# Attention over a long cache with a token mixer, on one core: the sixteenth query tile of a pair of heads loaded in six, six and four rows, and for two more pairs

## The chip, the core and the metric

The kernel runs on one core of one Trainium2 chip. The metric is the device time of one execution in microseconds (us), as the median of several executions. The core has engines for matrix products (PE, with PEld for its weight loads), for vectors (DVE), for activations (ACT), a general one (POOL), and a queue engine (SP) that issues nearly all loads from the chip's memory (HBM) into the on-chip memory. A load is carried out by up to 16 DMA engines side by side. The on-chip memory and the matrix results both have 128 rows, called partitions.

## The reference

Two layers, each an attention block with a residual and a mixer over one token with a residual. The batch is 2, one new token per batch entry, the width D is 512, and the cache holds 32768 positions for 8 key/value heads of 128 elements; four query heads share each of them. All data are 32-bit floats.

```python
q = (x @ wq).reshape(B, Sq, 32, 128).transpose(0, 2, 1, 3)
scores = einsum("bhqd,bhkd->bhqk", q, repeat(k_cache, 4)) * 128 ** -0.5
o = einsum("bhqk,bhkd->bhqd", softmax(scores), repeat(v_cache, 4))
attention = o.transpose(0, 2, 1, 3).reshape(B, Sq, 4096) @ wo
h = layernorm(y); u = gelu(einsum("bsd,sf->bdf", h, w1) + b1)
mixer = (einsum("bdf,fs->bds", u, w2) + b2).transpose(0, 2, 1)
# per layer: x = x + attention(layernorm(x)); x = x + mixer(layernorm(x))
```

The two caches are 268 MB each, and each layer reads both, apart from the parts that the kernel keeps on chip between the layers.

## The kernel before

**Units and chunks.** A unit is one layer, one batch entry and one key/value head (`units`, 32 in all). A unit's keys and values are read in chunks of 4096 positions (2 MB); usually four chunks come in one load of 8 MB (128 rows of 64 KB), so that a unit has two loads of keys and two of values. The script (`load_only`, `use`, `through`, `usual`) lists loads and uses in one fixed order: four key chunks of unit n, four value chunks of unit n-1, and so on. One use of a chunk is one step of the kernel's own clock (t); `kbeg[n]` is the step at which unit n's keys begin. `at(time, f, ...)` hangs any other work on such a step, so all orders are fixed when the program is built, and every engine runs its instructions in that order. SP waits, in order, for the buffer of the next load to come free (cells 0 to 7 of `mem`, of 16 KB in each partition).

**Weights.** The query and output weights of two neighbouring heads (`TWO_HEADS`, pairs 0 to 3) come in one load into two cells from `WCELL0 + k % 2 * 2` on (`load_weights`, L115 to L122), ten steps before the first unit of the pair. A head has four query tiles and four output tiles of 128 x 512 values, that is 256 KB each; a pair has 16 tiles, 4 MB. In layer 0 the pairs come as 0, 1, 2, 3 (pair 3 holds head 6, `single`, and the keeper, head 7); in layer 1 head 6 comes first, with a load of its own (L1069), and then pairs 0, 1, 2.

**The low tile.** For the pairs in `PART`, 1 and 2, the fourth query tile of the pair's first head is left out of that load, which then has 15 tiles (3840 KB). Its 128 rows of weights are laid out differently in HBM (`_two_heads`): 32 rows of 2048 values (8 KB), each of which holds four of the 128 rows. They go to partitions 0 to 15 and 32 to 47 of cell 8 (`lower_tile`, L124 to L135), after DVE has cleared these 48 partitions (L130). Each pair takes eight loads of four rows, the rows four apart (`u`, `u + 4`, `u + 8`, `u + 12`), spread over steps 46 to 18 before the pair, one every four steps. `lower_input` (L137) gathers the matching input columns, once a layer, and `low_products` (L148) forms the four products of 48 rows that take the place of the one product of 128 rows in `q_products` (L311). `make_q` (L329) turns the finished query row into the columns that the key products read.

**The change of layers.** Between the layers (`changes`, `change_of_layer`) the keeper's units run with many small loads, some data stay on chip, and cells 8 to 12 hold keys and values for a time; the last key chunks of unit (1, 0, 6) lie in cells 8 and 9. Pair 0 of layer 1 is opened at the first unit after the two of head 6.

Of the kernel before, what the change touches and what calls it, by code (L numbers as in the profile page):

```python
# [13 lines left out]
P = 128  # L14
CK = 4096
# [7 lines left out]
BANKS = 3  # L23
KEPT_Q = 4
TWO_HEADS = ((0, 1), (2, 3), (4, 5), (6, 7))
PART = (1, 2)
Q = 16
SIXTEENS = (0, 1, 4, 5)
PIECES = (32, 16, 8, 4, 4)
THIN = 16  # L30
QT = 4
# [9 lines left out]
def gqa_mixer_kernel(ctx: ExitStack, tc: tile.TileContext, x, kt, v, wqo, cols, out):  # L41
# [17 lines left out]
    nc = tc.nc  # L59
    B, D = out.shape  # L60
# [4 lines left out]
    R = wqo.shape[2] // (4 * D)  # L65
    DT = D // P
# [28 lines left out]
    WCELL0, WCELLS = 9, 4  # L95
# [3 lines left out]
    home = {}  # L99
    mem = const.tile([P, (WCELL0 + WCELLS) * CK + REST * QT * DH], F32, name="mem")  # L100
# [4 lines left out]
    lowered = {}  # L105
    low, first_half = (sm["ln"][: 3 * Q, 16 + k : 16 + k + w] for k, w in ((0, len(SIXTEENS) * B), (len(SIXTEENS) * B, 1)))

# [4 lines left out]
        w = home[h] + (DT - (h in lowered)) * D  # L112
        return mem[:, w : w + W].rearrange("p (t c) -> p t c", t=R)

    def load_weights(k, cell, n=2):  # L115
        tiles = n * (DT + R) - (k in PART)
        for j in range(n):
            home[TWO_HEADS[k][j]] = cell * CK + j * (DT + R - (k in PART)) * D
        of = wqo[k]
        if k in PART:  # L120
            of = of.rearrange("p c -> (p c)")[: P * tiles * D].rearrange("(p c) -> p c", p=P)
        nc.sync.dma_start(mem[:, cell * CK :][:, : tiles * D], of[:, : tiles * D])  # L122

    def lower_tile(k, step):  # L124


        w = len(SIXTEENS) * D
        to = mem[: 3 * Q, (WCELL0 - 1) * CK + PART.index(k) * w :][:, :w]
        if step < 0:
            nc.vector.memset(to, 0.0)  # L130
            return
        lowered[TWO_HEADS[k][0]] = to
        of = wqo[k].rearrange("p c -> (p c)")[-P * D :].rearrange("(u c) -> u c", u=2 * Q)
        a, u = divmod(step, 4)
        nc.sync.dma_start(to[2 * Q * a + u : 2 * Q * a + Q : 4], of[Q * a + u : Q * a + Q : 4])  # L135

    def lower_input():  # L137


        p = misc()  # L140
        for j, a in enumerate(SIXTEENS):
            nc.tensor.matmul(
                p[: 3 * Q, j * B : (j + 1) * B], ident[:, a * Q : (a + 3) * Q], sm["xn"][:, -B:], start=True, stop=True
            )
        nc.vector.tensor_reduce(first_half, mask[: 3 * Q, :], axis=AX.X, op=ALU.add)
        nc.vector.tensor_scalar_mul(low, p[: 3 * Q, : len(SIXTEENS) * B], first_half)

# [151 lines left out]
    def unit_of(n):  # L299

        return units[n]
# [74 lines left out]
    def load(is_v, n, c, m, places=None):  # L376
# [7 lines left out]
        for t in bufs:  # L384
            for w in [w * P for w in PIECES] if last else (t.shape[-1],):
                nc.sync.dma_start(t[:, :w], src[:, f : f + w])
# [533 lines left out]
    n = X0  # L920
# [40 lines left out]
    n = Y1 + 1  # L961
# [12 lines left out]
    kbeg, k_done, vbeg, v_done, vend_of, t = {}, {}, {}, {}, {}, 0  # L974
# [16 lines left out]
    def at(time, f, *a, rank=1, **k):  # L991
        done.setdefault(time, []).append((rank, f, a, k))

    HC = NCH // HALVES
    opens = {two[0]: k for k, two in enumerate(TWO_HEADS)}
# [92 lines left out]
    for n in range(NU):  # L1088
        layer, b, h = unit_of(n)
        kend, vend = kend_of[n], vend_of[n]  # L1090
        ahead = vend_of[n - 1] if n else 0
        if n and not X0 < n <= Y1 + 1:
            q0 = kbeg[n] - 6
            q1, q2, q3 = q0 + 1, q0 + 2, q0 + 2
            apart = n != X0 and h not in opens
            if apart and layer == 1:
                at(kbeg[n] - 11, make_q, n, 4)
                at(q0, make_q, n, 5)
                at(q1, make_q, n, 6)
            else:  # L1100
                at(kbeg[n] - 11 if apart else q0, make_q, n, 0)
                at(q1, make_q, n, 1)
            at(q2, make_q, n, 2)
            at(q3, make_q, n, 3)
        if n and h in opens and b == 0 and h != single or units[n] == (0, 0, single):
            at(kbeg[n] - 10, load_weights, opens[h], WCELL0 + opens[h] % 2 * 2)
            if opens[h] in PART:
                at(kbeg[n] - 55, lower_tile, opens[h], -1)
                for step in range(8):
                    at(kbeg[n] - 46 + 4 * step, lower_tile, opens[h], step)  # L1110
                if opens[h] == PART[0]:
                    at(kbeg[n] - 17, lower_input)
                at(kbeg[n] - 11, low_products, n, 0, 1)
                at(kbeg[n] - 10, low_products, n, 2, 3)
        if not X0 < n <= Y1:
            last = n == NU - 1
            e = kend + 2
            t0 = max(k_done[n, HC - 1], *(v_done[n - 1, c] for c in range(HC) if n), 0)
            t1 = ahead if last else max(kend + 2, ahead + (2 if n == X0 else 4))
            at(max(kend, e - 1), max_1, n)  # L1120
            at(e, max_2, n)
            at(t0, turn_scores, n, 0)
            at(e, exponentials, n, 0)
            at(t1, turn_scores, n, 1)
            at(t1, exponentials, n, 1)
            at(t1 + (1 if last else 2), denominators, n)
        if n == NU - 1:
            at(t1 + 1, gelu_table)
            at(t1, last_rows, (layer, b))
            at(vend, last_out, n)  # L1130
            at(vend, last_mixer, n)
            continue
        if X0 <= n < Y1:
            continue
        assert vbeg[n + 1] >= vend
        at(min(vend + 1, vbeg[n + 1]), out_0, n)
        at(min(vend + 1, vbeg[n + 1]), out_1, n)
        at(vend if n == NU - 2 else vend + 2, out_2, n)
        if n == X0 - 1:
            at(vend + 2, fold_rows)  # L1140
        key = (layer, b)
        if units[n] == [u for u in units if u[:2] == key][-1]:
            at(vend, mix_1, key)
            at(vend + 2, take_rows, key, row_tile())
            at(vend + 3, mix_2, key)
            at(vend + 1, gelu_table)
            begin = vend + 3
            exps = [kend_of[m] + 2 for m in (n + 1, n + 2)]
            exps += [max(e, vend_of[m] + 4) for e, m in zip(exps, (n, n + 1))]
            when = [w for w in range(begin, begin + FT + 1 + len(exps)) if w not in exps][: FT + 1]  # L1150
            e = when.pop()
            for f, w in enumerate(when):
                at(w + 1, hidden_out, key, f, rank=0)
                at(w, hidden_tile, key, f, rank=2)
            at(e, take_rows, key, None, rank=2)
            at(e + 1, mix_4, key)
# [26 lines left out]
def _two_heads(two, parted, d):  # L1183

    import numpy as np

    if not parted:
        return np.concatenate(two, axis=1)
    c = np.arange((d // P - 1) * d, d // P * d)
    main = np.concatenate([np.delete(two[0], c, axis=1), two[1]], axis=1)  # L1190
    last = two[0][:, c]
    low = [np.concatenate([last[16 * a + u : 16 * a + u + 16] for a in SIXTEENS], axis=1) for u in (0, 32)]
    return np.concatenate([a.ravel() for a in (main, *low)]).reshape(P, -1)


def _layout(A_x, A_k_cache, A_v_cache, A_wq, A_wo, B_w1, B_b1, B_w2, B_b2):

    import numpy as np

    B, HKV, SK, DH = A_k_cache.shape  # L1200
    D = A_x.shape[-1]
    n = SK // CK


    keys = np.arange(SK).reshape(n, CK)
    for c0, m in GROUPS:
        keys[c0 : c0 + m] = keys[c0 : c0 + m].reshape(P, m, CK // P).transpose(1, 0, 2).reshape(m, CK)
    k = keys.reshape(n // PACK, PACK // 2, 2, NG, 32, JT // QT, QT // SUB, SUB)
    k = k.transpose(0, 1, 6, 7, 3, 2, 5, 4).reshape(n, CK)
    kt = np.empty((B * HKV, SK * DH), A_k_cache.dtype)  # L1210
    for u, a in enumerate(A_k_cache.reshape(B * HKV, SK, DH)):
        for c0, m in GROUPS:
            kt[u, c0 * CK * DH : (c0 + m) * CK * DH] = a[k[c0 : c0 + m].ravel()].T.ravel()
    wq = A_wq.reshape(D // P, P, HKV, -1).transpose(2, 1, 0, 3)
    wo = A_wo.reshape(HKV, -1, DH, D).transpose(0, 2, 1, 3)
    wqo = np.concatenate([wq.reshape(HKV, P, -1), wo.reshape(HKV, DH, -1)], axis=2)
    w2 = B_w2.reshape(P, -1)
    w2 = np.stack([np.zeros_like(w2), w2], axis=2)
    cols = [a.reshape(P, -1) for a in (B_w1, B_b1, w2)] + [np.broadcast_to(B_b2.reshape(1, 1), (P, 1))]
    return {  # L1220
        "x": np.ascontiguousarray(A_x.reshape(B * (D // P), P).T),
        "kt": kt,
        "v": A_v_cache.reshape(B * HKV, SK * DH),
        "wqo": np.stack([_two_heads([wqo[h] for h in two], k in PART, D) for k, two in enumerate(TWO_HEADS)]),
        "cols": np.concatenate(cols, axis=1),
    }

# [24 lines left out]
```

## Time and profile before

| | |
|---|---|
| three executions | 2483.12, 2483.34 (median), 2483.51 us |
| the profiled execution's own time | 2483.2 us |
| its span, first to last instruction | 2481.4 us |
| PE, DVE, ACT busy | 55%, 10%, 7% of the span |
| read from HBM | 1059.10 MB, 427 GB/s over the span |
| weight loads | 3 of 4096 KB, 4 of 3840 KB, 1 of 2048 KB, 32 of 32 KB |

How to read it: "busy" counts an engine's own instructions. The queue part of the page gives the packets of each DMA queue, their bytes, and the time that they took as a share of what 16 DMA engines have in the span. A row of a timeline gives the start in us from the span's start, the duration, the engine, the line, the operation with output and inputs, the count of instructions that were merged, and in brackets the idle time before it with what ended that idle time: "9.69 <-DMA mem<-in_kt_dram" is 9.69 us idle, ended by the landing of keys. SPq is SP's queue; its rows are the moments at which a load is issued, not the time of the transfer.

### The profile page before, as it was taken

What the parts mean: (1) busy time and instruction counts of PE and PEld (TensorE: products, weight loads), DVE (VectorE), ACT (ScalarE), POOL (GpSimd) and SP (SyncE); (2) the same over time, 40 slices, a digit from 0 to 9 for tenths busy, and PEclk for the clock granted to TensorE, in tenths of its full rate; (3) what the DMA queues carried; (4) which work ended last, traced back from release to release, by engine and by line L of the source; (5) the groups of instructions that cost most, each with busy time, mean ns of one, the idle gap of its engine ahead of it and who ended that gap; (6) DMA issues with size and microseconds to landing.
All of it is one profiled execution on the core that took longest, in us unless ns stands there. A gap on an engine that the chain in (4) does not pass through costs nothing.

```text
span 2481.4 us, 20712 instructions
## 1 busy us (share of the span) xinstructions
PE 1375.6 (55%) x9414; PEld 375.6 (15%) x9414; DVE 257.8 (10%) x665; ACT 185.7 (7%) x546; POOL 4.9 (0%) x17
## 2 busy tenths in 40 slices
PE   4545545556555455466788454555455454456556
PEld 1111111111111111111222111111111111111112
DVE  1000000000000000010334000000000000010002
ACT  0000000000000000000212000000000000011002
POOL 0000000000000000000000000000000000000000
PEclk8777777776777777778899877777777777777778
DMA  9999999999999999999999999999999999999996
GB/s 422 435 430 427 439 432 431 433 432 430 435 430 432 436 425 436 434 433 421 415 418 426 433 434 436 430 435 433 428 433 428 437 429 434 432 433 429 432 434 293
DMA packets 27570, 1060.44 MB, mean 427 GB/s; under 512 B 3413, under 2 KB 3417, under 8 KB 4570
## 3 DMA queue, kind: packets, MB, share of 16 engines
q1 hardware_dynamic: 27192, 1059.08, 99.2%
q8 instruction: 74, 1.21, 0.2%
q14 instruction: 14, 0.11, 0.0%
q10 hardware_dynamic: 290, 0.04, 0.0%
HBM read 1059.10 MB, written 0.00 MB: 427 GB/s over the span
## 4 chain that ended last, share of the span: by engine, by line
DMA 72%; PE 26%; DVE 1%; issue 0%; another core or an unknown queue 0%; ACT 0%; SPq 0%; POOL 0%; DVEq 0%; ACTq 0%
DMA mem<-in_v_dram 69%; PE acc L516 21%; DMA mem<-in_kt_dram 3%; PE score L417 2%; PE kept L155 1%; PE kept L321 0%; DVE acc L798 0%; PE small L548 0%; PE small L444 0%; PE bcast L417 0%; PE small L686 0%; PE small L438 0%; PE bcast L321 0%; PE kept L738 0%
## 5 line engine op out<-in xcount | busy, mean ns | idle before, releaser
L417 PE MATMUL score<-mem,small_sb 128*32 128x512 f32 x4032 | 600.1, 721 | 575.3 <-DMA mem<-in_kt_dram 574.5
L516 PE MATMUL acc<-mem,S 128*16 128x512 f32 x4088 | 602.5, 722 | 474.4 <-DMA mem<-in_v_dram 472.7
L417 PEld LDWEIGHTS score<-mem,small_sb 128*32 128x32 f32 x4032 | 139.2, 127 | 948.9 <-DMA mem<-in_kt_dram 595.0
L455 ACT ACTIVATE S<-S,small_sb 128x128 f32<-128x128 f32 x236 | 121.5, 518 | 2076.0 <-DVE small_sb L446 1417.1
L516 PEld LDWEIGHTS acc<-mem,S 128*16 128x16 f32 x4088 | 130.8, 108 | 812.3 <-issue 727.8
L430 DVE TENSOR_REDUCE small_sb<-score 128x1 f32<-128x512 f32 x63 | 43.6, 692 | 757.1 <-PE score L417 757.1
L450 DVE STREAM_TRANSPOSE S<-score 128x512 f32<-128x512 f32 x63 | 44.8, 711 | 131.2 <-PE acc L516 127.0
L321 PE MATMUL kept<-mem,small_sb 128*2 128x512 f32 x104 | 55.5, 655 | 1.7 <-DVE small_sb L267 1.7
L239 PE MATMUL kept<-mem,small_sb 128*1 128x512 f32 (+1 forms) x252 | 44.9, 599 | 2.6 <-ACT mem L781 2.4
L455 ACT ACTIVATION_READ_ACCUMULATOR S<-S,small_sb 128x1 f32 x236 | 44.1, 187 | 0.0
L440 DVE TENSOR_REDUCE small_sb<-small 1x4 f32<-1x128 f32 x32 | 8.9, 279 | 324.5 <-PE small L438 324.5
L550 DVE RECIPROCAL small_sb<-small 128x4 f32<-128x4 f32 x32 | 5.9, 185 | 311.6 <-PE small L548 311.6
L569 DVE TENSOR_TENSOR small_sb<-small,small_sb 128x4 f32<-128x4 f32 x30 | 4.9, 164 | 307.2 <-PE small L558 307.2
L486 DVE SCALAR_TENSOR_TENSOR S<-acc,small_sb,S 128x128 f32<-128x128 f32 x96 | 33.7, 351 | 3.4
L347 PE MATMUL small<-small_sb,mem 2*128 2x2 f32 x120 | 16.0, 251 | 19.3 <-DVE mem L343 19.3
L484 DVE TENSOR_SCALAR S<-acc,small_sb 128x128 f32<-128x128 f32 x32 | 11.2, 350 | 112.7 <-PE acc L516 112.7
L558 PEld LDWEIGHTS small<-small_sb,S 128*128 128x128 f32 x64 | 13.2, 258 | 49.6 <-issue 42.0
L347 PEld LDWEIGHTS small<-small_sb,mem 2*128 2x128 f32 x120 | 14.7, 189 | 33.3 <-DVE mem L343 30.0
L155 PE MATMUL kept<-mem,small_sb 48*2 48x512 f32 x32 | 18.7, 711 | 0.0
L438 PE MATMUL small<-small_sb 128*1 128x128 f32 x64 | 16.8, 357 | 3.0 <-DVE small_sb L436 3.0
L558 PE MATMUL small<-small_sb,S 128*128 128x4 f32 x64 | 16.0, 320 | 3.9 <-DVE S L486 3.9
L686 PE MATMUL small<-small_sb 128*128 128x128 f32 x102 | 16.9, 297 | 0.0
(177 smaller groups left out, 343.5 us busy)
## 6 DMA issues: line engine op xcount, KB each, us to landing
mem<-in_v_dram SPq DMA_DIRECT2D x13, 2048.0 KB
mem<-in_kt_dram SPq DMA_DIRECT2D x20, 1024.0 KB
mem<-in_kt_dram SPq DMA_DIRECT2D x4, 4096.0 KB
mem<-in_wqo_dram SPq DMA_DIRECT2D x4, 3840.0 KB
mem<-in_v_dram SPq DMA_DIRECT2D x15, 1024.0 KB
mem<-in_wqo_dram SPq DMA_DIRECT2D x3, 4096.0 KB
mem<-in_v_dram SPq DMA_DIRECT2D x3, 4096.0 KB
mem<-in_kt_dram SPq DMA_DIRECT2D x1, 6144.0 KB
```

The lines of the kernel that those rows point to most:

```text
L155: nc.tensor.matmul(q_ps[n][:B, :], low[:, j * B : (j + 1) * B], lowered[h][:, j * D : (j + 1) * D], start=(j == 0), stop=False,)
L239: nc.tensor.matmul((rows if to is None else to)[32 * g : 32 * g + b + 1, :], weights if b else weights[:, 1:], row, start=to is not None, ...
L321: nc.tensor.matmul(q_ps[n][:m, :], xnT[:, d, b : b + m], wq_at(h, d), start=(d == 0 and h not in lowered), stop=(d == last),)
L347: nc.tensor.matmul(pt[:, r * m : (r + 1) * m], q_row[n][:m, r * DH : (r + 1) * DH], ident[:m, :m], start=True, stop=True,)
L417: nc.tensor.matmul(sc_ps[n, half][32 * g : 32 * g + 32, :], q, kc[k * NG + g], start=first, stop=last,)
L430: nc.vector.tensor_reduce(mx[n][:, half : half + 1], sc_ps[n, half], axis=AX.X, op=ALU.max)
L450: nc.vector.transpose(S[half][:, :w], sc_ps[n, half][:, :w])
L455: nc.scalar.activation(s[:, :, h], s[:, :, h], AF.Exp, bias=neg[n][:, h : h + 1], scale=SCALE, accum_out=lsum[n][:, half, h : h + 1],)
L486: nc.vector.scalar_tensor_tensor(t, acc[:, k * DH : (k + 1) * DH], mask[:, k : k + 1], t, op0=ALU.mult, op1=ALU.add)
L516: nc.tensor.matmul(acc[32 * g : 32 * g + R * QT, :], S[half][:, col : col + R * QT], vc[q], start=((n, c) in v_first and q < NG), stop=((n ...
L558: nc.tensor.matmul(po[:, :R], blocks[n], selh, start=True, stop=True)
L686: nc.tensor.matmul(p[:, :P], ident, ident, start=True, stop=True)
```

## The change

`PART` becomes pairs 1, 2 and 3. The low tile's 16 rows on each side are loaded as rows 0 to 5, 6 to 11 and 12 to 15, neighbouring rows in each load (`SPLIT`), so a pair takes six loads of 6, 6, 4, 6, 6 and 4 rows.

Pair 3 has its low tile in layer 0, and pair 0 in layer 1. Pair 0 of layer 0 and head 6 of layer 1 keep the whole load; so two pairs are needed in both layouts, and HBM gets second copies of pairs 0 and 3 (`COPIES`, `source`). The 15-tile load is now put at the end of its two cells, not at the start. Of cell 8, odd pairs take the second half and even pairs the first.

For pair 0 of layer 1 (`near`) the places differ: DVE's clearing 16 steps before the pair, the six loads at steps 15, 14, 13, 11, 10 and 9 before, the low products at 4 and 3.5 before, the other three query products and the turning of the query at 3, 2.5, 2 and 1.5 before.

```diff
-PART = (1, 2)
+PART = (1, 2, 3)
+COPIES = (0, 3)
+SPLIT = ((0, 6), (6, 12), (12, 16))
...
-    def load_weights(k, cell, n=2):
-        tiles = n * (DT + R) - (k in PART)
+    def source(k, whole):
+
+        if whole == (k not in PART):
+            return wqo[k]
+        return wqo[len(TWO_HEADS) + COPIES.index(k)]
+
+    def load_weights(k, cell, n=2, whole=True):
+
+        tiles = n * (DT + R) - (not whole)
+        to = (cell + n) * CK - tiles * D
         for j in range(n):
-            home[TWO_HEADS[k][j]] = cell * CK + j * (DT + R - (k in PART)) * D
-        of = wqo[k]
-        if k in PART:
+            home[TWO_HEADS[k][j]] = to + j * (DT + R - (not whole)) * D
+        of = source(k, whole)
+        if whole:
+            lowered.pop(TWO_HEADS[k][0], None)
+        else:
             of = of.rearrange("p c -> (p c)")[: P * tiles * D].rearrange("(p c) -> p c", p=P)
-        nc.sync.dma_start(mem[:, cell * CK :][:, : tiles * D], of[:, : tiles * D])
+        nc.sync.dma_start(mem[:, to:][:, : tiles * D], of[:, : tiles * D])
...
-        to = mem[: 3 * Q, (WCELL0 - 1) * CK + PART.index(k) * w :][:, :w]
+        to = mem[: 3 * Q, (WCELL0 - 1) * CK + k % 2 * w :][:, :w]
...
-        of = wqo[k].rearrange("p c -> (p c)")[-P * D :].rearrange("(u c) -> u c", u=2 * Q)
-        a, u = divmod(step, 4)
-        nc.sync.dma_start(to[2 * Q * a + u : 2 * Q * a + Q : 4], of[Q * a + u : Q * a + Q : 4])
+        of = source(k, False).rearrange("p c -> (p c)")[-P * D :].rearrange("(u c) -> u c", u=2 * Q)
+        a, u = divmod(step, len(SPLIT))
+        u0, u1 = SPLIT[u]
+        nc.sync.dma_start(to[2 * Q * a + u0 : 2 * Q * a + u1], of[Q * a + u0 : Q * a + u1])
...
+            near = layer == 1 and opens.get(h) == 0 and b == 0
             q0 = kbeg[n] - 6
             q1, q2, q3 = q0 + 1, q0 + 2, q0 + 2
+            if near:
+                q0, q1, q2, q3 = (kbeg[n] - k / 2 for k in (6, 5, 4, 3))
...
-            at(kbeg[n] - 10, load_weights, opens[h], WCELL0 + opens[h] % 2 * 2)
-            if opens[h] in PART:
-                at(kbeg[n] - 55, lower_tile, opens[h], -1)
-                for step in range(8):
-                    at(kbeg[n] - 46 + 4 * step, lower_tile, opens[h], step)
-                if opens[h] == PART[0]:
+            k = opens[h]
+            whole = k == 0 and layer == 0
+            at(kbeg[n] - 10, load_weights, k, WCELL0 + k % 2 * 2, whole=whole)
+            if not whole:
+                at(kbeg[n] - (16 if near else 55), lower_tile, k, -1)
+                for step in range(2 * len(SPLIT)):
+                    i = step + step // len(SPLIT)
+                    at(kbeg[n] - 15 + i if near else kbeg[n] - 46 + 4 * step, lower_tile, k, step)
+                if k == 1 - layer:
                     at(kbeg[n] - 17, lower_input)
-                at(kbeg[n] - 11, low_products, n, 0, 1)
-                at(kbeg[n] - 10, low_products, n, 2, 3)
+                at(kbeg[n] - (4 if near else 11), low_products, n, 0, 1)
+                at(kbeg[n] - (3.5 if near else 10), low_products, n, 2, 3)
```

**SP, layer 0, ahead of pair 3.** Before, the rows up to the weights of pair 3 (the last row) are:

```order
L386 DMA mem<-in_kt_dram 128x16384
L386 DMA mem<-in_v_dram 128x16384
L386 DMA mem<-in_kt_dram 128x16384
L386 DMA mem<-in_v_dram 128x16384
L122 DMA mem<-in_wqo_dram 128x8192
```

Now, from the fourth of the six low loads on, there stands:

```order
L148 DMA mem<-in_wqo_dram 6x2048
L399 DMA mem<-in_kt_dram 128x16384
L148 DMA mem<-in_wqo_dram 6x2048
L399 DMA mem<-in_v_dram 128x16384
L148 DMA mem<-in_wqo_dram 4x2048
L399 DMA mem<-in_kt_dram 128x16384
L399 DMA mem<-in_v_dram 128x16384
L399 DMA mem<-in_kt_dram 128x16384
L399 DMA mem<-in_v_dram 128x16384
L134 DMA mem<-in_wqo_dram 128x7680
```

Six low loads have come in between the loads of keys and values, and the load of the pair's weights has 7680 values a row instead of 8192.

**SP, layer 1, ahead of pair 0.** Before, after the last key chunks of unit (1, 0, 6) (the three loads of 128x8192), there stands:

```order
L386 DMA mem<-in_kt_dram 128x8192 x3
L386 DMA mem<-in_kt_dram 128x16384
L386 DMA mem<-in_v_dram 128x16384
L122 DMA mem<-in_wqo_dram 128x8192
L386 DMA mem<-in_kt_dram 128x16384
L386 DMA mem<-in_v_dram 128x16384
```

Now:

```order
L399 DMA mem<-in_kt_dram 128x8192 x3
L399 DMA mem<-in_kt_dram 128x16384
L148 DMA mem<-in_wqo_dram 6x2048 x2
L148 DMA mem<-in_wqo_dram 4x2048
L399 DMA mem<-in_v_dram 128x16384
L148 DMA mem<-in_wqo_dram 6x2048
L134 DMA mem<-in_wqo_dram 128x7680
L148 DMA mem<-in_wqo_dram 6x2048
L148 DMA mem<-in_wqo_dram 4x2048
L399 DMA mem<-in_kt_dram 128x16384
L399 DMA mem<-in_v_dram 128x16384
```

Three low loads have come ahead of a value load, in whose issue SP must therefore first wait for DVE's clearing of cell 8.

**PE, layer 1, the query of pair 0's first unit.** Before, the four query products (L321) and the turning of the row (L347) stand among the last key products of the unit ahead (score_86):

```order
L417 MATMUL score_86<-mem,small_sb 32x512 x16
L321 MATMUL kept_82<-mem,small_sb 2x512 x2
L417 MATMUL score_86<-mem,small_sb 32x512 x8
L321 MATMUL kept_82<-mem,small_sb 2x512 x2
L417 MATMUL score_86<-mem,small_sb 32x512 x8
L347 MATMUL small<-small_sb,mem 128x2 x4
L516 MATMUL acc<-mem,S_90 16x512 x8
```

Now they stand among its last value products (acc), and the four low products (L168) ahead of them:

```order
L430 MATMUL score_86<-mem,small_sb 32x512 x32
L168 MATMUL kept_82<-mem,small_sb 2x512 x2
L529 MATMUL acc<-mem,S_90 16x512 x4
L168 MATMUL kept_82<-mem,small_sb 2x512 x2
L529 MATMUL acc<-mem,S_90 16x512 x4
L451 MATMUL small<-small_sb 1x128
L334 MATMUL kept_82<-mem,small_sb 2x512 x2
L529 MATMUL acc<-mem,S_90 16x512 x4
L334 MATMUL kept_82<-mem,small_sb 2x512
L529 MATMUL acc<-mem,S_90 16x512 x4
L457 MATMUL small<-small_sb 128x4
L529 MATMUL acc<-mem,S_90 16x512 x4
```

The query's work has moved behind the landing of the unit's last values, and the turning of the row follows the last of these rows.

More of the change, by code (lines that the diff above doesn't have):

```diff
@@ L113, in wo_at @@
         return mem[:, w : w + W].rearrange("p (t c) -> p t c", t=R)
-    def load_weights(k, cell, n=2):
-        tiles = n * (DT + R) - (k in PART)
-        for j in range(n):
-            home[TWO_HEADS[k][j]] = cell * CK + j * (DT + R - (k in PART)) * D
-        of = wqo[k]
-        if k in PART:
+    def source(k, whole):
[5 more added lines that the diff above has]
+        to = (cell + n) * CK - tiles * D
+        for j in range(n):
+            home[TWO_HEADS[k][j]] = to + j * (DT + R - (not whole)) * D
[3 more added lines that the diff above has]
+        else:
             of = of.rearrange("p c -> (p c)")[: P * tiles * D].rearrange("(p c) -> p c", p=P)
-        nc.sync.dma_start(mem[:, cell * CK :][:, : tiles * D], of[:, : tiles * D])
+        nc.sync.dma_start(mem[:, to:][:, : tiles * D], of[:, : tiles * D])
     def lower_tile(k, step):
         w = len(SIXTEENS) * D
-        to = mem[: 3 * Q, (WCELL0 - 1) * CK + PART.index(k) * w :][:, :w]
+        to = mem[: 3 * Q, (WCELL0 - 1) * CK + k % 2 * w :][:, :w]
         if step < 0:
+            lowered[TWO_HEADS[k][0]] = to
             nc.vector.memset(to, 0.0)
             return
-        lowered[TWO_HEADS[k][0]] = to
-        of = wqo[k].rearrange("p c -> (p c)")[-P * D :].rearrange("(u c) -> u c", u=2 * Q)
-        a, u = divmod(step, 4)
-        nc.sync.dma_start(to[2 * Q * a + u : 2 * Q * a + Q : 4], of[Q * a + u : Q * a + Q : 4])
+        of = source(k, False).rearrange("p c -> (p c)")[-P * D :].rearrange("(u c) -> u c", u=2 * Q)
+        a, u = divmod(step, len(SPLIT))
+        u0, u1 = SPLIT[u]
+        nc.sync.dma_start(to[2 * Q * a + u0 : 2 * Q * a + u1], of[Q * a + u0 : Q * a + u1])
     def lower_input():
@@ L1223, in _layout @@
         "v": A_v_cache.reshape(B * HKV, SK * DH),
-        "wqo": np.stack([_two_heads([wqo[h] for h in two], k in PART, D) for k, two in enumerate(TWO_HEADS)]),
+        "wqo": np.stack(
+            [
+                _two_heads([wqo[h] for h in TWO_HEADS[k]], parted, D)
+                for k, parted in [(k, k in PART) for k in range(len(TWO_HEADS))] + [(k, k not in PART) for k in COPIES]
+            ]
+        ),
         "cols": np.concatenate(cols, axis=1),
```

## The prediction

> **What bounds the kernel now.** I read the engine table and the queues first, then the chain, then the places where PE waits for loads.
>
> ```profile
> span 2481.4 us, 20712 instructions
> PE 1375.6 (55%) x9414; PEld 375.6 (15%) x9414; DVE 257.8 (10%) x665; ACT 185.7 (7%) x546; POOL 4.9 (0%) x17
> q1 hardware_dynamic: 27192, 1059.08, 99.2%
> q8 instruction: 74, 1.21, 0.2%
> DMA 72%; PE 26%; DVE 1%; issue 0%; another core or an unknown queue 0%; ACT 0%; SPq 0%; POOL 0%; DVEq 0%; ACTq 0%
> ```
>
> SP's queue, q1, keeps 16 DMA engines busy for 99.2% of the span, 2461.5 us each on average. Keys and values are read whatever the change does, so it can only alter how evenly these engines finish. The last landing shows how much there is to gain:
>
> ```profile
> 2463.75 1.06 PE L532 MATMUL kept<-mem,S 128*4 128x128 f32 x24 [0.24 <-DMA mem<-in_v_dram]
> 2465.06 0.40 PE L532 MATMUL kept<-mem,S 128*4 128x128 f32 x8 [0.25 <-DMA mem<-in_v_dram]
> 2478.88 0.58 SPq L769 DMA_DIRECT2D out_dram<-mem  x1
> ```
>
> The last wait for values ends at 2465.1 us, 3.6 us after the average engine's 2461.5. That is the most that better sharing could save (0.14%); the 16 us behind it are the closing mixer, which the change doesn't touch. So **a large gain is ruled out**.
>
> From the queue's row one engine moves 1059.08 MB / (16 x 2461.5 us) = 26.9 KB per us: 0.305 us for a row of 8 KB, and 0.61 us for its sixteenth of a 256 KB tile.
>
> **What the low loads cost now.** They go with every key and value load of a stretch. PE's waits for keys, in a stretch of layer 0 with a low load to every load, and in a later one without:
>
> ```profile
> 393.52 3.64 PE L417 MATMUL score<-mem,small_sb 128*32 128x512 f32 x16 [9.69 <-DMA mem<-in_kt_dram]
> ...
> 550.92 3.64 PE L417 MATMUL score<-mem,small_sb 128*32 128x512 f32 x16 [10.03 <-DMA mem<-in_kt_dram]
> ...
> 637.49 3.62 PE L417 MATMUL score<-mem,small_sb 128*32 128x512 f32 x16 [8.80 <-DMA mem<-in_kt_dram]
> ...
> 753.64 6.57 PE L417 MATMUL score<-mem,small_sb 128*32 128x512 f32 x44 [7.33 <-DMA mem<-in_kt_dram]
> ```
>
> The first two rows are four pairs of loads apart: 39.35 us a pair. The last two are three pairs apart: 38.72. The difference, 0.63 us, is that of two low loads: 0.317 us each, one 8 KB row on one engine (0.305 above). I read two things from it. A load of four rows uses four engines, one row each; and in this stretch those engines are the last of the sixteen, so what they carry is the pace. In layer 1 it begins otherwise:
>
> ```profile
> 1570.63 3.64 PE L417 MATMUL score<-mem,small_sb 128*32 128x512 f32 x16 [9.44 <-DMA mem<-in_kt_dram]
> ...
> 1609.34 5.80 PE L417 MATMUL score<-mem,small_sb 128*32 128x512 f32 x32 [9.37 <-DMA mem<-in_kt_dram]
> ...
> 1648.24 3.42 PE L417 MATMUL score<-mem,small_sb 128*32 128x512 f32 x16 [9.08 <-DMA mem<-in_kt_dram]
> ...
> 1687.31 9.51 PE L417 MATMUL score<-mem,small_sb 128*32 128x512 f32 x64 [10.10 <-DMA mem<-in_kt_dram]
> ```
>
> 38.71, 38.90 and 39.07 us: the first low loads are free, because other engines are later there, and then they come onto the path.
>
> **The change part by part.** *Rows and tiles.* Per layer it goes from two pairs with eight low loads to three with six. The engines that carry a row of every load pay 18 x 0.317 = 5.71 us, not 5.07: +0.63. All sixteen lose a sixteenth of one tile: -0.61. So the engines now last come out at **+0.02 us a layer**, and those without low rows at -0.61. What the layer gains depends on who is last at its end: +0.02 if it is the four engines of the low rows all along, -0.61 if others are. Over two layers that is +0.04 to -1.22. I take -0.3, near the upper end, since the rows of layer 0 have the low engines last.
>
> [...]
>
> *The two new engines.* If six rows use six engines, two that carried none get a row of four loads a pair: 24 x 0.317 = 7.6 us, less 1.2. The four get 36 x 0.317 = 11.4. The two stay hidden if what else they carry is under 3.8 us more than the four have. I take it as hidden; the price if it isn't is the second rival below.
>
> *A load of neighbouring rows.* The trace has no load whose rows are neighbours on fewer than 128 partitions. The nearest is the load of four rows, 0.317 us; from below, nothing makes a row cheaper than an engine's 0.305. From above, rows that take turns at one part of the memory cost a multiple (third rival). I take 0.317, the row of the same kind, and keep the other end.
>
> *SP.* Its own time is small:
>
> ```profile
> L135 SPq DMA_DIRECT2D mem<-in_wqo_dram x32: 599/600/737, 42.1 to 1845.4; - x32
> ```
>
> 36 issues instead of 32 are 2.4 us more of SP, spread over the run, each beside the 9 to 10 us that PE waits for a landing anyway. Only ahead of layer 1's pair 0 does a low load add a wait:
>
> ```profile
> 1379.29 0.33 SPq L386 DMA_DIRECT2D mem<-in_kt_dram  x1
> 1381.01 0.33 SPq L386 DMA_DIRECT2D mem<-in_v_dram  x1
> 1390.60 0.33 SPq L122 DMA_DIRECT2D mem<-in_wqo_dram  x1
> 1390.61 0.69 DVE L430 TENSOR_REDUCE small_sb<-score 128x1 f32<-128x512 f32 x1 [8.28 <-PE score L417]
> 1404.84 3.64 PE L417 MATMUL score<-mem,small_sb 128*32 128x512 f32 x16 [14.31 <-DMA mem<-in_kt_dram]
> 1414.63 0.33 SPq L386 DMA_DIRECT2D mem<-in_kt_dram  x1
> 1425.36 9.06 PE L516 MATMUL acc<-mem,S 128*16 128x512 f32 x64 [9.25 <-DMA mem<-in_v_dram]
> ...
> L130 DVE MEMSET mem<- x4: 1765/1765/1765, 26.2 to 1678.4; 48x2048 f32 x4
> ```
>
> DVE's clearing comes behind the reduction that ends at 1391.3, so the first low load goes out at 1391.3 + 1.77 = 1393.1. Three at 0.6 us, and the value load follows at 1395.0 instead of 1381.0, with the weights and the rest behind it. The key load ahead of it is still landing until 1404.8, so its place in the engines' queues is filled some 9 us before they need it: nothing on the path. If the cover were gone, each us beyond those 9 would delay every later landing.
>
> *PE and DVE.* Products of the low tile:
>
> ```profile
> L155 PE MATMUL kept<-mem,small_sb x32: 587/589/1054, 252.2 to 1922.6; 48*2 48x512 f32 x32
> ...
> L321 PE MATMUL kept<-mem,small_sb x104: 592/592/1061, 17.2 to 2028.7; 128*2 128x512 f32 x104
> ```
>
> A pair has eight records of the low products and saves two of the others: 6 x 0.59 = 3.5 us of PE, twice, and two more clearings of 1.77 us on DVE. Both lie in PE's waits for landings (9.7 and 9.4 us in the rows above). Layer 1's later query, now behind the last values of the unit ahead, ends in a copy and four small products before the next keys, whose landing PE waits for in any case: nothing.
>
> The sum is 2483.2 (the profiled execution: 2481.4 of span and 1.8 around it) - 0.3 = **2482.9 us**. The median of the runs, 2483.34, is 0.14 above that execution, which is within the range.
>
> **The rivals.** *First, the low engines are never last at the ends.* Then both layers give the whole 0.61: 2482.0. For it speaks the free beginning of layer 1; against it the stretch of layer 0. It is part of my range and sign.
>
> *Second, the two new engines become last.* The instruction packets of q8 take 0.2% of 16 engines' span, 79 us for 74, 1.07 each, on the same engines. Spread over the twelve without low rows they are 6.6 us each; on eight of them, 9.9. The new engines then stand at 7.6 + 6.6 = 14.2 or 17.5 against the four's 11.4: +2.8 to +6.1, 2486.0 to 2489.3. For it: the fetches go somewhere, and the stretch of layer 0 shows that they aren't what ends last there. Against: the twelve needn't share them alike, and two that carry none stay hidden at 7.6.
>
> *Third, neighbouring rows take turns*, the case that ends slower. [...] It decides as soon as a neighbouring row costs over 0.5 us on the path, for then 36 of them outweigh the 0.2% that a measurement of this kernel can tell from no change. For it: the loads of before keep their rows four apart. Against: no row shows two engines slowing each other. [...]
>
> *Fourth, the six rows don't spread over six engines* but over three, two each: a pair costs 4 x 0.63 + 2 x 0.32 = 3.2 us, 9.5 a layer against 5.1, less 0.6: +3.8 twice, 2490.8. That the change would not do what it says has only this against it: the four rows did spread over four.
>
> *Fifth, the wait in layer 1 eats its 9 us*, through a later clearing: 1 to 5 us, up to 2488.
>
> **How the numbers follow.** Forecast with the first rival 0.70, second 0.08, third 0.17, fourth 0.03, fifth 0.02. The forecast's own range is 2481.5 to 2484. The range reaches down to the 2482.0 of the first rival less 1 us for how instruction packets fall, 2481.0, and up to the end of the second, 2489.5; the third and fourth, 0.20, are left out. Faster by over 0.2% (under 2478.4) is beyond the 3.6 us that there are: 0.02 for a misreading. Slower (over 2488.3): third and fourth, with a part of the second: 0.21. Within: 0.77.
>
> **What would show it.** Right: six weight loads of 3840 KB and 36 low ones; in layer 0's stretches with low loads some 39.35 us to a pair of loads, now also ahead of pair 3; the value load of 1381 issued near 1395 and landing as before. Wrong: a pair of loads there at 40 us or more (rows in turn), PE waiting longer than 10 us for the values of 1425, or a later stretch over 38.7 us without any low load.

## The result, and the profile after

The changed kernel takes **2504.16 us** (median of five runs, 2503.25 to 2504.96), the kernel before 2483.51 in the same comparison (2483.12 to 2485.03). The ratio is 1.0082, with a 95% interval of 1.007 to 1.0093: 20.6 us slower. The prediction said 2482.9, range 2481.0 to 2489.5. It was wrong; the time lies beyond the range, on the side of its third rival.

The page of the changed kernel, with the lines that answer to those of before (span, engines, queues, the chain):

```profile
span 2502.4 us, 20749 instructions
PE 1389.1 (56%) x9426; PEld 376.2 (15%) x9426; DVE 261.3 (10%) x667; ACT 185.7 (7%) x546; POOL 4.9 (0%) x17
q1 hardware_dynamic: 27320, 1059.08, 98.9%
q8 instruction: 74, 1.21, 0.2%
DMA 71%; PE 27%; DVE 1%; issue 1%; another core or an unknown queue 0%; ACT 0%; SPq 0%; ACTq 0%; DVEq 0%
```

The bytes are the same and the queue is nearly as full as before, so its packets themselves took longer: 98.9% of 2502.4 is 2474.9 us of each engine where it was 2461.5, on average over all sixteen. These 13.4 of the 21.0 us by which the span grew are no matter of sharing out; in the rest engines stood idle. The end, from the timelines of PE and SP:

```profile
2484.52 1.07 PE L545 MATMUL kept<-mem,S 128*4 128x128 f32 x24 [0.23 <-DMA mem<-in_v_dram]
2485.84 0.40 PE L545 MATMUL kept<-mem,S 128*4 128x128 f32 x8 [0.25 <-DMA mem<-in_v_dram]
...
2499.64 0.61 SPq L782 DMA_DIRECT2D out_dram<-mem  x1
```

The last values are there at 2485.8 instead of 2465.1, 20.8 us later; what follows takes as long as before. So the whole loss lies in the stream of loads. PE's waits for keys in the timeline, for the stretch of layer 0 with pair 2's low loads and for a later one:

```profile
396.47 3.60 PE L430 MATMUL score<-mem,small_sb 128*32 128x512 f32 x16 [8.84 <-DMA mem<-in_kt_dram]
...
517.31 9.77 PE L430 MATMUL score<-mem,small_sb 128*32 128x512 f32 x64 [9.84 <-DMA mem<-in_kt_dram]
...
556.02 3.64 PE L430 MATMUL score<-mem,small_sb 128*32 128x512 f32 x16 [10.05 <-DMA mem<-in_kt_dram]
...
642.74 3.35 PE L430 MATMUL score<-mem,small_sb 128*32 128x512 f32 x16 [9.07 <-DMA mem<-in_kt_dram]
...
681.46 8.76 PE L430 MATMUL score<-mem,small_sb 128*32 128x512 f32 x56 [9.83 <-DMA mem<-in_kt_dram]
```

396.47 to 517.31 are three pairs of loads, **40.28 us a pair**; the prediction had set "40 us or more (rows in turn)" as a sign that it is wrong. After the last low load it is 38.71 at once (517.31 to 556.02), and 38.72 later on: here the stream loses time beside the low loads, and no longer behind them. Layer 1's first pair, in the timelines of DVE, SP and PE, is in the order forecast, some 11 us later:

```profile
1402.74 1.76 DVE L143 MEMSET mem<- 48x2048 f32 x1 [0.37 <-issue]
1404.57 0.96 SPq L148 DMA_DIRECT2D mem<-in_wqo_dram  x3
1405.57 0.35 SPq L399 DMA_DIRECT2D mem<-in_v_dram  x1
1416.49 3.65 PE L430 MATMUL score<-mem,small_sb 128*32 128x512 f32 x16 [14.88 <-DMA mem<-in_kt_dram]
1437.25 3.62 PE L529 MATMUL acc<-mem,S 128*16 128x512 f32 x16 [9.54 <-DMA mem<-in_v_dram]
```

From the keys' landing to the values' it is 20.76 us, where it was 20.52 (1404.84 to 1425.36): the value load that SP held back lands in its turn.

The trace also keeps every packet of the queue. A row of 64 KB of keys or values is one packet. Counted for the stretch 385 to 556 us, in which both kernels load pair 2's low tile: packets of 64 KB that took over 25 ns more than the median (2421 ns in both), out of those that began within 2.5 us of a low load's first packet, one entry for each low load:

```
before   0/33 0/32 0/32 0/32 0/32 0/33 0/32 0/32
after    4/33 23/33 9/31 13/32 22/31 14/32
```

Before, a low load disturbs no packet of the stream; the only slow ones (4 in the stretch) stand alone, beside an instruction fetch. After, up to 23 of 33 are slowed. At the first low load of all (six rows, at 70.4 us) these are the sixteen packets of 64 KB that began between 69.9 and 70.9 us, with their durations in ns:

```
2902 2896 2892 2892 2892 2904 2899 2900 3262 2891 2896 2895 2945 2896 3029 2901
```

Each lasts longer than the stretch in which they began, so they are on sixteen different engines, of which the low load of six rows uses six (its six packets, each of 309 to 314 ns, begin within 194 ns of each other): the disturbance reaches the others too.

### The profile page after: what moved, and what is told of

Read it like the earlier page. It is cut to its first block, busy times and chain, and to the rows that moved or that the text cites. A ratio compares the mean times of both kernels' runs of the same rounds, so it can differ in the third digit from the quotient of the medians.

```text
span 2502.4 us, 20749 instructions
## 1 busy us (share of the span) xinstructions
PE 1389.1 (56%) x9426; PEld 376.2 (15%) x9426; DVE 261.3 (10%) x667; ACT 185.7 (7%) x546; POOL 4.9 (0%) x17
## 3 DMA queue, kind: packets, MB, share of 16 engines
q1 hardware_dynamic: 27320, 1059.08, 98.9%
## 4 chain that ended last, share of the span: by engine, by line
DMA 71%; PE 27%; DVE 1%; issue 1%; another core or an unknown queue 0%; ACT 0%; SPq 0%; ACTq 0%; DVEq 0%
DMA mem<-in_v_dram 67%; PE acc L529 21%; DMA mem<-in_kt_dram 3%; PE score L430 2%; PE kept L168 1%; PE kept L334 1%; DVE acc L811 0%; PE small L561 0%; PE small L457 0%; PE bcast L430 0%; PE small L451 0%; ACT mem L773 0%; PE bcast L334 0%; PE kept L252 0%
## 5 line engine op out<-in xcount | busy, mean ns | idle before, releaser
L529 PE MATMUL acc<-mem,S 128*16 128x512 f32 x4088 | 611.0, 729 | 490.3 <-DMA mem<-in_v_dram 488.6
L168 PE MATMUL kept<-mem,small_sb 48*2 48x512 f32 x48 | 31.9, 798 | 0.0
```

The costliest lines, as they stand in the source:

```text
L168: nc.tensor.matmul(q_ps[n][:B, :], low[:, j * B : (j + 1) * B], lowered[h][:, j * D : (j + 1) * D], start=(j == 0), stop=False,)
L529: nc.tensor.matmul(acc[32 * g : 32 * g + R * QT, :], S[half][:, col : col + R * QT], vc[q], start=((n, c) in v_first and q < NG), stop=((n ...
```

## The experiments

Each run is compared with the kernel before on the same chip (2483.5 to 2484.1 in the comparisons; intervals are 95%). None leaves out any part of the computation. The diffs show the lines that matter; "..." stands for lines left out.

**Pairs or split.** First the two halves of the change apart. The changed kernel with loads of four rows, four partitions apart:

```diff
-SPLIT = ((0, 6), (6, 12), (12, 16))
+SPLIT = 4
...
-        nc.sync.dma_start(to[2 * Q * a + u0 : 2 * Q * a + u1], of[Q * a + u0 : Q * a + u1])
+        nc.sync.dma_start(to[2 * Q * a + u : 2 * Q * a + Q : SPLIT], of[Q * a + u : Q * a + Q : SPLIT])
```

> The changed kernel with all its parted pairs and its near schedule, but with low loads of four rows that lie four partitions apart (eight loads per pair), as before the change. Theory A (the neighbouring rows cost the time): the extra pairs cost their rows alone, in each layer 24 rows x 0.317 - 0.61 - 5.07 = +1.9 us at the low engines, of which layer 1's first pair may hide: 2485 to 2488 us, and no stretch of layer 0 with low loads above 39.6 us per pair of loads. Theory B (the two extra pairs, the whole loads that now end elsewhere, or layer 1's near schedule cost the time): 2500 to 2505 us, as the changed kernel.

2488.57 us, ratio 1.0021 (1.0011 to 1.003): +5.0 of the 20.6 us. Its waits for keys in the timeline, the first and the last of pair 2's stretch:

```profile
393.62 3.64 PE L429 MATMUL score<-mem,small_sb 128*32 128x512 f32 x16 [8.64 <-DMA mem<-in_kt_dram]
...
551.03 3.58 PE L429 MATMUL score<-mem,small_sb 128*32 128x512 f32 x16 [9.00 <-DMA mem<-in_kt_dram]
```

157.41 us for four pairs of loads is 39.35, to the digit what the kernel before has. Theory A holds; the time is 0.6 us above its range. The mirror image is the kernel before with the new split alone:

```diff
+SPLIT = ((0, 6), (6, 12), (12, 16))
...
-        a, u = divmod(step, 4)
-        nc.sync.dma_start(to[2 * Q * a + u : 2 * Q * a + Q : 4], of[Q * a + u : Q * a + Q : 4])
+        a, u = divmod(step, len(SPLIT))
+        u0, u1 = SPLIT[u]
+        nc.sync.dma_start(to[2 * Q * a + u0 : 2 * Q * a + u1], of[Q * a + u0 : Q * a + u1])
```

> The kernel before with its own two pairs, and only the split changed: loads of six, six and four neighbouring rows, not of four rows four apart. Theory A (the neighbouring rows cost the time): four half-layers of low loads at +2.0 to +2.6 us each per pair and layer, so 4 x (4.6 to 5.1 less 2.5) = +8 to +10 us, 2491 to 2494 us, and layer 0's stretch with low loads near 40.3 us per pair of loads, not 39.35. Theory B (the pairs): 2481 to 2484 us, and 39.35 us or less.

2494.23 us, 1.0042 (1.0028 to 1.0056): +10.7. The same waits:

```profile
396.69 3.64 PE L419 MATMUL score<-mem,small_sb 128*32 128x512 f32 x16 [9.81 <-DMA mem<-in_kt_dram]
...
517.53 8.80 PE L419 MATMUL score<-mem,small_sb 128*32 128x512 f32 x64 [10.80 <-DMA mem<-in_kt_dram]
556.25 3.64 PE L419 MATMUL score<-mem,small_sb 128*32 128x512 f32 x16 [9.34 <-DMA mem<-in_kt_dram]
```

40.28 us a pair of loads, then 38.72, as in the changed kernel. Four pairs cost 10.7 us, so six would cost 16.0; the changed kernel lies 15.6 above the pairs-only run. The two halves add up.

**One extra pair at a time.** The pairs-only kernel without layer 1's parted pair, and without layer 0's:

```diff
-            near = layer == 1 and opens.get(h) == 0 and b == 0
+            near = False
...
-            whole = k == 0 and layer == 0
+            whole = k == 0
...
```

> The pairs-only kernel (2488.6 us) without its parted pair in layer 1: of the two extra pairs only heads 6 and 7 in layer 0 are parted, layer 1 is as before. Account by engines: 8 rows x 0.317 - 0.61 = +1.9 us at the low engines, 2485 to 2486.5 us. If all of the pairs' 5 us lies in layer 1's near schedule: 2483 to 2484.5 us.

2485.57 us, 1.0007 (0.9997 to 1.0016): +1.7, the account's +1.9, though the interval takes in no change at all.

```diff
-            whole = k == 0 and layer == 0
+            whole = k == 0 and layer == 0 or k == 3
```

> The pairs-only kernel (2488.6 us) without its parted pair in layer 0: only heads 0 and 1 in layer 1 are parted, with the near schedule. Account by engines: +1.9 us at the low engines, 2485 to 2486.5 us. If the near schedule itself costs (its wait, its clearing, its low loads in two close bunches): 2486.5 to 2488 us.

2486.83 us, 1.0011 (1.0001 to 1.002): +3.0, 1.1 more than the account and within the bounds given for a near schedule that costs. Whether that is the near schedule or only the measurement stays open. 1.7 and 3.0 make 4.7 of the 5.0 of both.

**The count of six, or neighbours.** Four neighbouring rows to a load, in eight loads (the split-only run with another `SPLIT`):

```diff
+SPLIT = ((0, 4), (4, 8), (8, 12), (12, 16))
```

> The kernel before with its own two pairs and its eight loads of four rows, but each load takes four neighbouring rows to four neighbouring partitions. Theory A1 (neighbouring rows wait for each other, the more there are in sum the more it costs; all 32 rows of a pair lie in groups of four): as dear as the six, six, four split or more, +8 to +15 us, 2491 to 2498 us. Theory A2 (what costs is the count of six, which is spread over six engines of 16, or the fewer and larger loads): 2482 to 2485 us.

2497.77 us, 1.0057 (1.0042 to 1.0072): +14.2, more than six, six and four. And six rows that lie four apart, with the two rows left over in a load of their own, on a low tile of 32 partitions. The diff is against the eight-engines run, which is shown further down; the eight loads of a pair again come every four steps:

```diff
-        nc.sync.dma_start(to[step::4], of[step::4])
+        a, u = divmod(step, 2)
+        rows = slice(a, a + 24, 4) if u == 0 else slice(a + 24, 2 * Q, 4)
+        nc.sync.dma_start(to[rows], of[rows])
```

> The kernel before with its two pairs and the low tile on 32 partitions, as in the eight-engines run, but in loads of six and of two rows that lie four apart (engines 0 and 1 carry eight rows of a pair, 2 to 5 four). Theory P (a count of six costs nothing if no rows are neighbours): 2482.5 to 2489 us, the upper end if engines 4 and 5 pay for instruction fetches as in the eight-engines run, and no slowed packets beside the low loads. Theory A2 (a count of six is spread badly): 2492 us or more, with slowed packets.

2489.15 us, 1.0019 (1.0009 to 1.0029). No packet is slowed by a load of six: 0/32 0/33 0/32 0/32 in pair 2, against 4/32 16/32 6/32 8/32 beside the loads of two. So the count is not to blame, and that the loads of two disturb the stream was in neither theory; the time lies just above the 2489 of theory P. What the 5.1 us are is told below with the eight-engines run, whose layout it has.

**Where the rows come from, or where they go.** The host permutes the rows of the low tile, so that four that lie apart in main memory go to neighbouring partitions, or the reverse:

```diff
-        nc.sync.dma_start(to[2 * Q * a + u : 2 * Q * a + Q : 4], of[Q * a + u : Q * a + Q : 4])
+        nc.sync.dma_start(to[2 * Q * a + 4 * u : 2 * Q * a + 4 * u + 4], of[Q * a + u : Q * a + Q : 4])
...
+    low = [a.reshape(4, 4, -1).swapaxes(0, 1).reshape(16, -1) for a in low]
```

> The kernel before with its two pairs and loads of four rows, where the four rows of a load go to neighbouring partitions but come from rows four apart in the chip's main memory (the host lays them out so). Theory P (four writes to one group of neighbouring partitions are what costs): slow as the four-neighbours run, which took 2497.8, so 2495 to 2500 us, with slowed 64 KB packets on all engines beside each low load. Theory M (reading a run of neighbouring rows from main memory is what costs): as before, 2482.5 to 2485 us.

2497.7 us, 1.005 (1.0035 to 1.0065): +13.6. And the reverse:

```diff
-        nc.sync.dma_start(to[2 * Q * a + u : 2 * Q * a + Q : 4], of[Q * a + u : Q * a + Q : 4])
+        nc.sync.dma_start(to[2 * Q * a + u : 2 * Q * a + Q : 4], of[Q * a + 4 * u : Q * a + 4 * u + 4])
...
+    low = [a.reshape(4, 4, -1).swapaxes(0, 1).reshape(16, -1) for a in low]
```

> The mirror image: the four rows of a load come from one run of neighbouring rows in main memory and go to partitions four apart. Theory P (the partitions): as before, 2482.5 to 2485 us, with no slowed packets beside the low loads. Theory M (main memory): 2495 to 2500 us.

2483.77 us, 0.9998 (0.9989 to 1.0008). The waits for keys of the first of the two, and of the second, at the two ends of pair 2's stretch:

```profile
397.01 3.64 PE L417 MATMUL score<-mem,small_sb 128*32 128x512 f32 x16 [9.69 <-DMA mem<-in_kt_dram]
...
558.08 3.64 PE L417 MATMUL score<-mem,small_sb 128*32 128x512 f32 x16 [10.07 <-DMA mem<-in_kt_dram]
```

```profile
393.67 3.64 PE L417 MATMUL score<-mem,small_sb 128*32 128x512 f32 x16 [8.76 <-DMA mem<-in_kt_dram]
...
551.07 3.46 PE L417 MATMUL score<-mem,small_sb 128*32 128x512 f32 x16 [9.11 <-DMA mem<-in_kt_dram]
```

161.07 us against 157.40: 40.27 a pair of loads and 39.35. Of the two theories P holds: going to neighbouring partitions costs 13.6 us, and coming from neighbouring rows of main memory nothing that shows (-0.3 us).

**Neighbours, or engines.** Rows two apart:

```diff
+        u = 8 * (u // 2) + u % 2
-        nc.sync.dma_start(to[2 * Q * a + u : 2 * Q * a + Q : 4], of[Q * a + u : Q * a + Q : 4])
+        nc.sync.dma_start(to[2 * Q * a + u : 2 * Q * a + u + 7 : 2], of[Q * a + u : Q * a + u + 7 : 2])
```

> The kernel before with its two pairs and loads of four rows, two partitions apart instead of four, so that two of them lie in one group of four partitions (0 and 2, 4 and 6). Theory P with groups of four partitions: two at a time cost less than four, between before and the four-neighbours run, 2485 to 2493 us. Theory of touching rows alone (only partitions that touch disturb each other): as before, 2482.5 to 2485 us. If it takes any two in a group to bring the whole cost: 2495 to 2500 us.

2491.68 us, 1.0029 (1.0018 to 1.0039): no two rows touch, and it still costs 7.6, within the first theory's bounds. The eight-engines run had looked for a gain, with 32 partitions and loads of eight rows four apart, four rows of a pair to each of eight engines instead of eight to each of four:

```diff
-SIXTEENS = (0, 1, 4, 5)
+SIXTEENS = (0, 2, 4, 6)
...
-        nc.sync.dma_start(to[2 * Q * a + u : 2 * Q * a + Q : 4], of[Q * a + u : Q * a + Q : 4])
+        nc.sync.dma_start(to[step::4], of[step::4])
...
-                for step in range(8):
-                    at(kbeg[n] - 46 + 4 * step, lower_tile, opens[h], step)
+                for step in range(4):
+                    at(kbeg[n] - 46 + 8 * step, lower_tile, opens[h], step)
...
```

> The kernel before with its own two pairs, the low tile laid on partitions 0 to 31 (one block of 32 rows, no clearing) and loaded in four loads of eight rows that lie four apart. Theory A (only neighbours cost): eight engines carry four rows of a pair each, 4 x 0.317 = 1.27 us and not 2.54, so 4 x 1.27 = 5 us less at the low engines where they are last; the whole stays within what the packets allow, 2480 to 2484 us. Theory A2 (a load spread over other than four engines costs): above 2488 us.

2488.21 us, 1.0017 (1.0008 to 1.0027): 4.6 us slower, the bound of theory A2, but not for its cause, since 0/32 0/33 0/33 0/32 packets are slowed beside the low loads. In its timeline the time is lost far from any low load, in single steps. PE's waits for keys, of the eight-engines run and then of before:

```profile
996.64 9.13 PE L414 MATMUL score<-mem,small_sb 128*32 128x512 f32 x64 [10.31 <-DMA mem<-in_kt_dram]
...
1036.87 3.64 PE L414 MATMUL score<-mem,small_sb 128*32 128x512 f32 x16 [9.77 <-DMA mem<-in_kt_dram]
```

```profile
996.64 8.39 PE L417 MATMUL score<-mem,small_sb 128*32 128x512 f32 x64 [9.36 <-DMA mem<-in_kt_dram]
...
1035.38 3.64 PE L417 MATMUL score<-mem,small_sb 128*32 128x512 f32 x16 [9.76 <-DMA mem<-in_kt_dram]
```

40.23 us where before has 38.74: a step of 1.49. In the packet records an instruction fetch begins at 1000.9 and takes 1.03 us, and the 64 KB packet that it meets takes 0.55 more, 1.6 together. Such steps come again near 714, 2019 and 2290, behind the fetches of 704.1, 2005.4 and 2285.3.

The packet records can say whether the engine has low rows. While the queue is full, a packet begins 3 or 4 ns before an earlier one ends, so the packets fall into sixteen chains, as many as there are engines. A record doesn't name its engine, and the engine numbers in the expectations are names only. In the kernel before, the low rows of pair 2 are on four chains, eight on each. The durations of the fetches repeat every eight, as if they went to eight engines in turn (from 416.6 us on 1018, 1018, 1073, 1068, 1060, 1107, 1099 and 1095 ns, then 1018, 1018, 1073 and 1069 again). The four fetches at the steps stand whole rounds of eight apart from each other and from the one of 416.6 us; by that they are on one engine, and at 416.6 its chain carries low rows of pair 2. In the load before the step at 1000.9 that engine ends 0.04 us ahead of the last one; from the fetch on it is the last, and the load ends 1.50 us later. In the kernel before, none of the four fetches of pair 2's stretch is on a chain with low rows, and the engine of the fetch at 1001.0 is some 5 us ahead of the last. So in the eight-engines run, as far as the durations tell, an engine that has both low rows and fetches is now the last. The six-apart run has a step at the same place, and one of its six engines with low rows has fetches too (at 121.8 us). No run moves the fetches alone.

To part this from the layout on 32 partitions, eight loads of four rows eight apart; loads of four rows are on four chains in the kernel before (the diff is against the eight-engines run; the loads again come every four steps):

```diff
-        nc.sync.dma_start(to[step::4], of[step::4])
+        nc.sync.dma_start(to[step::8], of[step::8])
```

> The kernel before with its two pairs and the low tile on 32 partitions, in eight loads of four rows that lie eight apart, so that engines 0 to 3 alone carry them, eight rows a pair each, as before. Theory F (in the eight-engines and six-apart runs, 2488.2 and 2489.2 us, the low rows came onto engines that lose time to instruction fetches as well): here nothing is added, 2482.5 to 2485 us, and no step of 1.5 us in the landings outside the stretches with low loads. Theory L (the layout on 32 partitions itself costs, by its products or by the missing clearing): 2487 to 2490 us.

2492.48 us, 1.0034 (1.0021 to 1.0048): above both theories. Packets are slowed beside every low load, 22/32 23/32 19/32 17/32 20/31 23/32 23/32 26/31: rows eight apart slow the stream as neighbours do. So nearness isn't the cause. Nothing was slowed beside rows four apart that begin on partitions 0 to 3 (four, six or eight rows to a load) or 32 to 35 (four rows), but beside the six-apart run's loads of two rows, which go to partitions 24 to 31, packets were slowed at the same spacing. The last run sets the place against the spacing: rows four apart in loads of four, first to partitions 0 to 15 and then to 16 to 31 (again against the eight-engines run, with a load every four steps):

```diff
-        nc.sync.dma_start(to[step::4], of[step::4])
+        a, u = divmod(step, 4)
+        nc.sync.dma_start(to[Q * a + u : Q * a + Q : 4], of[Q * a + u : Q * a + Q : 4])
```

> The kernel before with its two pairs and the low tile on 32 partitions, in eight loads of four rows that lie four apart: the first four loads of a pair go to partitions 0 to 15, as before, the last four to partitions 16 to 31. Both halves have the same spacing and engines 0 to 3. [...] Theory D (the distance between the rows of a load decides, four apart is harmless): 2482.5 to 2485 us, and no slowed packets beside either half.

2489.38 us, 1.0022 (1.0012 to 1.0032): above theory D. The waits for keys of pair 2's stretch, and behind them the packets that are slowed at each of its eight low loads, by the trace of the same run:

```profile
394.75 3.65 PE L415 MATMUL score<-mem,small_sb 128*32 128x512 f32 x16 [9.39 <-DMA mem<-in_kt_dram]
434.09 7.26 PE L415 MATMUL score<-mem,small_sb 128*32 128x512 f32 x48 [8.92 <-DMA mem<-in_kt_dram]
473.62 3.64 PE L415 MATMUL score<-mem,small_sb 128*32 128x512 f32 x16 [9.81 <-DMA mem<-in_kt_dram]
513.62 8.47 PE L415 MATMUL score<-mem,small_sb 128*32 128x512 f32 x64 [9.61 <-DMA mem<-in_kt_dram]
553.36 3.64 PE L415 MATMUL score<-mem,small_sb 128*32 128x512 f32 x16 [10.38 <-DMA mem<-in_kt_dram]
```

```
eight_apart    22/32 23/32 19/32 17/32 20/31 23/32 23/32 26/31
next_engines   0/32 0/33 0/32 0/32 22/32 24/32 27/32 27/32
```

The first pair of loads takes 39.34 us, as before, and the second, in which the first low load to partitions 16 to 31 falls, 39.53. Those that follow take 40.00 and 39.74. By the chains, the low rows to partitions 16 to 31 are on the same four engines as those to 0 to 15 (433 to 473 us), and beside the fifth low load a packet is slowed on each of the sixteen. So theory D fails: with the same spacing on the same four engines, no packet is slowed beside the rows to 0 to 15, and 22 to 27 of 32 beside those to 16 to 31. Nor is it these partitions alone. The eight-engines run wrote them too, at the same spacing, with its low rows on eight chains, and slowed nothing. Two things differ for them between these runs, the engines that carry the rows and the rows in a load, four against eight; loads of four rows to 0 to 15 disturb nothing in this same run. No run parts the two for 16 to 31, and a packet's record names neither its engine nor its partitions: why the place costs is not shown.

What the low rows of each kernel cost, against before (for the changed kernel, against the pairs-only run):

| kernel | low rows | us | us a row |
|---|---|---|---|
| from neighbours (four apart) | 128 | -0.3 | 0 |
| next engines, the rows to 16 to 31 | 64 | 5.9 | 0.09 |
| two apart | 128 | 7.6 | 0.06 |
| eight apart | 128 | 8.6 | 0.07 |
| split only | 128 | 10.7 | 0.08 |
| changed kernel | 192 | 15.6 | 0.08 |
| four neighbours, to neighbours | 128 | 14.2, 13.6 | 0.11 |

Where the rows disturb the stream, a low row costs it 0.06 to 0.11 us, two apart the least and four neighbours the most. The eight-engines run (4.6 us, no packet slowed in pair 2's stretch) and the six-apart run (5.1 us) are not in the table, since their times hold the steps at fetches as well.

No version here beats the kernel before, and the account leaves none in sight: in the layout of before a further pair costs 1.9 us by it (1.7 and 3.0 in the runs), and on eight engines the rows met the steps shown above.

## Why the prediction was wrong

- **The bound** was right: q1 is still full, the last wait is for values, and nothing was to be gained beyond 3.6 us. But from it came "it can only alter how evenly these engines finish", and that was too narrow: the change made the packets of all engines slower.
- **A load of neighbouring rows** is the step that failed: "I take 0.317, the row of the same kind, and keep the other end." The row was not of the same kind. The low packets themselves still take 309 to 316 ns for the most part; it is the stream beside them that pays, 2.6 us more for a pair than with rows four apart (15.6 us over six pairs). In the trace of before no low load of pair 2 slows a packet (0 of 32 or 33 beside each), so it could not show this price.
- **The third rival** had the sign, and its own mark was passed: the stretch above shows (40.28 - 38.72) / 2 = 0.78 us for a low load, over the 0.5 that it set for a neighbouring row. The 5.1 us a pair that stand in the split-only run's expectation are shown by no run; pair 2's three pairs of loads lost 3 x 1.56 = 4.7. That rows take turns no run shows either: in the trace packets of all sixteen engines are slowed, and in the eight-apart run, where no rows are neighbours, 17 to 26 of some 32 beside each load. Its chance of 0.17 rested on "no row shows two engines slowing each other", which the trace of before could not have shown.
- **Rows and tiles**: the changed kernel can't show +0.02 us a layer under the larger loss. With eight four-row loads the account, 8 x 0.317 - 0.61 = +1.9 for a pair, came out at +1.7 in layer 0 and +3.0 in layer 1.
- **Six rows on six engines** was the author's estimate, since the trace of before shows only four rows on four, and it was right: the six packets of the changed kernel's first low load run at the same time, on six chains. The six-apart run's loads of six disturb nothing, and the fourth rival, three engines, isn't needed for any number.
- **The two new engines** were taken as hidden. The eight-engines run speaks against that: 16 rows, 5.1 us, on each of four more engines cost 4.6 us, though the four of before were relieved of as much. So the second rival (2486.0 to 2489.3) may have its mechanism too, with fetches on eight engines, as its dearer case had it and as the durations suggest; what it takes of the changed kernel's 20.6 us can't be told apart, since there all engines are late.
- **SP** and **layer 1's wait** were right: 36 low loads and six of 3840 KB, the clearing, three low loads and the value load in the order forecast (SP's three low issues took 1.0 us and not 1.8), and PE's wait for those values 9.54 us, under the 10 of the mark. The 36 issues are even cheaper than taken, see below.
- **PE and DVE** were right in kind: their additions stay within the waits, as the pairs-only run's unchanged 39.35 us a pair of loads shows.

## What to carry to other kernels

A small load beside a stream that fills all engines can cost the stream more than the load's own packets take: here, at the same bytes, it cost nothing or 5.9 to 15.6 us, by the partitions and rows of each load alone. Try another layout in a run before building on it, and read the cost in the stream's packets, not in the small load's. And where a trace holds only rows laid out with care, it has no price for another layout: take such a price from the end that a rival gives, or give the rival the greater chance.

## What the hardware showed beside that

- Beside the changed kernel's first low load, whose rows of 8 KB take 0.31 us each, packets of all sixteen engines are slowed. In the eight-apart run the packets of 64 KB that are slowed in pair 2's stretch sum to 25.8 us more than the median, before 2.0: 23.8 us for 32 low rows, 0.74 each, which is more than the row's own time. What slows them no run here shows.
- SP issued the changed kernel's loads to neighbouring partitions in 326 ns (median of 36), the loads of four rows four apart of before in 600. It goes by the destination here too: the run that goes to neighbours has 326, the one that only comes from neighbours 600.

```profile
L148 SPq DMA_DIRECT2D mem<-in_wqo_dram x36: 248/326/617, 42.8 to 1825.4; - x36
```
